# Sorted block attention and a gated feed-forward on one core: a written list of calls with one score block of chunks 3 and 4 a layer ahead, eight 64-row score blocks, and narrower warm-up products

## The chip, the cores and the metric

The kernel runs on one core of a Trainium2 chip. The metric is the device time of one execution, in microseconds (us); before the change the median of three runs is 238.9 us (238.58 to 239.17). The engines are named as the profile names them: PE (TensorE, the matmuls), PEld (its weight loads), DVE (VectorE), ACT (ScalarE), POOL (GpSimd) and SP (SyncE, here only a queue that issues transfers).

## The reference

Queries, keys and values are (4, 8, 768, 64): four batches, eight heads, 768 positions in 8 blocks of 96. A small matrix per head sorts (mixes) the key and value blocks, attention runs within each block of 96, and the result goes through a feed-forward layer with a cosine gate.

```python
P = sort_net                                  # (4, 8, 8, 8)
for _ in range(5):
    P = exp(P - max(P)); P /= sum over the last axis; P /= sum over the axis before
k_sorted = einsum('bhij,bhjcd->bhicd', P, k blocks)
v_sorted = einsum('bhij,bhjcd->bhicd', P, v blocks)
attn = softmax(q block @ k_sorted block.T / 8)     # 96 x 96, within a block
x    = (attn @ v_sorted block)                     # all heads: 3072 tokens x 512
h    = x @ w_in                                    # 512 -> 2048
out  = (h * cos(h)) @ w_out                        # 2048 -> 512
```

## The kernel before

The 3072 tokens are handled in eight chunks n = 0 to 7 of 384 tokens; a chunk has four units u = 0 to 3, each one block of 96 positions with all its eight heads. In the text a letter and the numbers n, u stand for one step; the list of calls after the change uses the same letters.

The feed-forward of a chunk, here called its layer, is eight up steps and twelve down quarters. An up step U n p (function `up`) is 8 products of 384 columns into PSUM, followed by C (the cosine on ACT, written as a sine with a bias) and G (the multiplication on DVE). A down quarter D n t q is 4 products of 512 columns (line 583); there are three row tiles t with four quarters each, then an eviction O and a store W. The time in which the down quarters run is called the layer's tail.

The attention of chunk n+1 is put between the products of layer n. For a unit: S, the scores, 8 products of 96 columns over 128 rows (line 405, in `qk`, or in halves of four products, `qk_half`); M, the row maximum, and X, its subtraction (DVE, lines 447 and 449); E, the exponential on ACT (`expo`, line 467) into one of three buffers `p_buf`; TD, a transpose by DMA on SP's queue into `pT` (or TP and TE: on PE with an eviction, `p_transpose`); AV, 8 products of 65 columns (`av_products`, line 514); N, a reciprocal and a multiplication on DVE (lines 525 and 527) giving `xn`; and XD, a transpose by DMA into the next layer's `xT` (or XP and XE on PE with an eviction, `x_transpose`, line 545).

The sorting of keys and values is made of products too: `ks` and kg (`k_sort_g`) for keys, vb (`v_sort_b`) and vg (`v_sort_g`, 128-column products) for values, each with an eviction (kge, vbe, vge). Two transfers on SP (kswap) exchange halves of the sorted keys.

PSUM is held in two pools: `big`, three buffers of two banks, and `acc`, two buffers of one bank. A buffer is given to the next tile that asks for it in the order of the program, so that a product waits for the reader of the tile that was there before: for a G, an X, an N or an eviction.

Nothing reorders the work at run time: each engine runs its instructions in the order of the program. Before the change, nested calls set this order: `moe_up` and `moe_down` take lists of calls (slots) that are made behind a step, for example

```python
    moe_up(3, [[(w_next,), (qk_half, 4, 0, 0)], [(w_next,)],
    ...
               [(w_next,), (qk_half, 4, 1, 1)], [(qk, 4, 2)]])
    moe_down(3, [[(qk, 4, 3), (expo, 4, 2)], [(w_next, A, *B), (qk, 5, 0), (expo, 4, 3)],
```

At the start, while inputs are loaded and the Sinkhorn iterations run on DVE and ACT, `keep_warm` issues products of zeros on PE (line 238).

Of the kernel before, what the change touches and what calls it, by code (L numbers as in the profile page):

```python
# [14 lines left out]
AX = mybir.AxisListType  # L15


@with_exitstack
def kernel(
# [15 lines left out]
    nc = tc.nc  # L35
# [199 lines left out]

    def keep_warm(times, t, cols=512):
        for _ in range(times):
            nc.tensor.matmul(  # L238
                t[:, :cols], warm[:], warm[:, :1].to_broadcast([128, cols]),
                start=True, stop=True)  # L240
# [131 lines left out]
    MH = H2 * IC  # L372

    def k_products(ps, t, c, rows, rhs, keys=kbuf):
        nc.tensor.matmul(  # L375
            ps[:, t], keys[rows, c * 2 * D:(c + 1) * 2 * D], rhs, start=True, stop=True)

    def k_sort_g(t0, eng, pool, tag):
        ps = pool.tile([128, 4, 4 * NB], FP32, name="ks", tag=tag)
        for t in range(4):  # L380
            k_products(ps, t, t0 + t, slice(0, 128), bds[1].rearrange("p x i -> p (x i)"),
                       pair)
# [25 lines left out]
    def v_cols(d, permuted):  # L408
        return vperm[:, d * blk:d * blk + 128] if permuted else vv[:, d]

    def v_sort_b(b, d0, nd, eng, pool, tag):
        ps = pool.tile([128, nd, 2 * NB], FP32, name="vs", tag=tag)
        rows, xs = slice(0, 64 + b * 64), slice(b * H, (b + 1) * H)
        for t in range(nd):
            nc.tensor.matmul(
                ps[:, t], v_cols(d0 + t, b == 1 or d0 + t >= D // 2)[rows],
                bdv[rows, xs].rearrange("p x i -> p (x i)"), start=True, stop=True)
        copy_on(
            eng, vS[0][:, b * 2 * NB:(b + 1) * 2 * NB, d0:d0 + nd],
            ps[:blk].rearrange("p t n -> p n t"))  # L420

    def v_sort_g(d0, nd, eng, pool, tag):
        ps = pool.tile([128, nd, 4 * NB], FP32, name="vs", tag=tag)
        for t in range(nd):
            nc.tensor.matmul(  # L425
                ps[:, t], v_cols(d0 + t, True), bds[1].rearrange("p x i -> p (x i)"),
                start=True, stop=True)
        copy_on(eng, vS[1][:, :, d0:d0 + nd], ps[:blk].rearrange("p t n -> p n t"))

    def v_at(g, b2, hp, h2, i):  # L430
        return (b2 * 2 + hp) * NB + h2 * nb + i


    LATE = 5
    s_t, pb, pT, xn_t = {}, {}, {}, {}
    xT = {}
    cnt = [0]

    def qk_part(n, u, part, pool, tag):
# [7 lines left out]
        nc.vector.reduce_max(mx[:], scv, axis=AX.X)  # L447
        s = s_t[n, u][:, part[0]:part[0] + w].rearrange("p e h c -> p (e h) c")
        nc.vector.tensor_tensor(s, scv, mx.to_broadcast(list(s.shape)), op=ALU.subtract)  # L449
# [12 lines left out]
    def expo(n, u, on_pe=False):
        p = p_bufs[cnt[0] % NP]
        cnt[0] += 1


        nc.scalar.activation(  # L467
            p[:, :, :blk], s_t.pop((n, u)).rearrange("p e h c -> p (e h) c"), AF.Exp,
            scale=scale)
        if n < LATE:  # L470
# [30 lines left out]

    def av_products(n, u):
        g, b2, ih = where(n)
        if n not in xT:
# [14 lines left out]
        av_ps[n, u] = a  # L519

    def av_norm(n, u, on_pe=False):
        avv = av_ps.pop((n, u))[:blk, :, :H2 * (D + 1)].rearrange(
# [3 lines left out]
        xn = small.tile([blk, H2, 2, D], BF16, name="xn", tag="xn")  # L526
# [3 lines left out]
        if on_pe:  # L530
            xn_t[n, u] = xn
        else:
            nc.sync.dma_start_transpose(
                out=xT[n][:, :, u * blk:(u + 1) * blk],
                in_=xn.rearrange("p h e d -> p (h e d)"))

    def x_transpose(n, u, eng, pool, tag, to=None):
        us = range(u, (u if to is None else to) + 1)
        ps = pool.tile([128, KC, len(us), blk], BF16, name="xps", tag=tag)

        turn = order[:] if n < NQ else ident[:blk, :blk]
        for i, z in enumerate(us):
            xn = xn_t.pop((n, z))
            for h2 in range(H2):
                nc.tensor.transpose(
                    ps[:, h2, i], xn[:, h2].rearrange("p e d -> p (e d)"), turn)
        copy_on(eng, xT[n][:, :, u * blk:us.stop * blk], ps.rearrange("p k i c -> p k (i c)"))

    gt = {}

    def up(n, fp):
        w = TC

        h = big.tile([128, 2, 512], FP32, name="h", tag="big")
        for f2 in range(2):
            f = fp * 2 + f2
            for kk in range(KC):
                nc.tensor.matmul(  # L558
                    h[:, f2, :w], w_in_t[:, kk, f * 128:(f + 1) * 128], xT[n][:, kk],
                    start=(kk == 0), stop=(kk == KC - 1))  # L560
        c = cosp.tile([128, 2, TC], FP32, name="c", tag="c")
        nc.scalar.activation(c[:], h[:, :, :w], AF.Sin, bias=half_pi[:, 0:1])  # L562
        if fp % 2 == 0:
# [3 lines left out]
            gt[n, fp // 2][:, f:f + 2], c[:], h[:, :, :w], op=ALU.mult)  # L567

    out_ps, kept = {}, {}

    def store(n, ts, o_s, eng=nc.sync):
        r0 = n * TC + ts * 128
        eng.dma_start(out=out[r0:r0 + 128, :], in_=o_s[:])

    def let_go(n, ts):
        store(n, ts, kept.pop((n, ts)))

    def down(n, ts, half, stores, mid=()):
        if half == 0:
            out_ps[ts] = acc.tile([128, Dm], FP32, name="o", tag="acc")  # L580
        o = out_ps[ts]
        for f in range(half * FC // 2, (half + 1) * FC // 2):
            nc.tensor.matmul(  # L583
                o[:], gt[n, f // 4][:, f % 4, ts * 128:(ts + 1) * 128], w_out_t[:, f, :],
                start=(f == 0), stop=(f == FC - 1))
            if f % (FC // 2) == FC // 4 - 1:
                step(mid)
        if half == 0:
            return
        if stores is None:  # L590

            z = (n % 2 * 3 + ts) * 2 * Dm
            o_s = vbuf[:, z:z + 2 * Dm].bitcast(FP32)
        else:
            o_s = op.tile([128, Dm], FP32, name="o_s", tag="o_s")
        late = n > 0 and ts == TC // 128 - 1
        copy_on(V if late else A, o_s[:], o[:])
# [542 lines left out]
```

## Time and profile before

| what | value |
|---|---|
| time, median of three runs | 238.9 us (238.58 to 239.17) |
| the profiled execution: its span | 236.9 us; no time of its own is given for it, so the 2.0 us between the span and the median stand for what lies around it |
| PE busy | 228.3 us, 96% of the span |
| DVE, ACT, POOL busy | 171.1 us (72%), 154.0 us (65%), 93.4 us (39%) |
| mean granted TensorE clock | 0.998 |
| layer 1's tail (72.82 to 87.91 us) | 15.09 us, PE busy 14.80 |
| layer 2's tail (100.43 to 115.54 us) | 15.11 us, PE busy 14.69 |
| layer 3's tail (128.63 to 142.54 us) | 13.91 us, PE busy 13.50 |

A row of the profile's timeline is "start, length, engine, line, operation, tile written <- tiles read, count", and in square brackets the idle time before it and what ended it. The modelled end of a matmul lies behind the start of the next, so that the real step of a product is the difference of two starts divided by the count between them, and a wait is what such a difference has beyond that.

### The profile page before, as it was taken

The numbers are of one execution on the slowest core, as the hardware profiler recorded it, in microseconds if no ns is written. First come the engines' busy times: TensorE is split into PE (matmuls) and PEld (weight loads), VectorE is DVE, ScalarE is ACT, GpSimd is POOL, SyncE is SP. The second block draws the span as 40 slices with busy tenths as digits, with TensorE's granted clock in tenths as the row PEclk, the third lists the DMA queues.
The fourth block names the chain that finished last, engine by engine and source line by source line (L and its number), as shares of the span: only waits on it lengthen the run. The fifth ranks groups of instructions, "written<-read, shape, count | busy, mean of one in ns | idle before, by whom it ended". The sixth has DMA issues, their size and how long they took to land.

```text
span 236.9 us, 5429 instructions
## 1 busy us (share of the span) xinstructions
PE 228.3 (96%) x2230; PEld 144.0 (61%) x2230; DVE 171.1 (72%) x284; ACT 154.0 (65%) x205; POOL 93.4 (39%) x117
## 2 busy tenths in 40 slices
PE   8699999999999999999999999999999999999994
PEld 2368799567665656655666556655564565555553
DVE  5658976887789666893689976998698769535700
ACT  3356975588889747795688747673767376646611
POOL 7699994894970098940808000800000000000000
PEclk9999999999999999999999999999999999999999
DMA  7999999995899989869899938944972460341012
GB/s 97 203 199 205 203 224 211 148 201 167 102 117 183 146 155 136 160 150 184 95 104 101 116 64 150 209 68 91 119 216 46 80 192 3 55 133 47 0 44 89
DMA packets 66423, 30.89 MB, mean 130 GB/s; under 512 B 55136, under 2 KB 61920, under 8 KB 66144
## 3 DMA queue, kind: packets, MB, share of 16 engines
q0 software_dynamic: 24048, 13.64, 42.1%
q1 hardware_dynamic: 42064, 16.73, 33.4%
q8 instruction: 17, 0.28, 0.5%
q10 hardware_dynamic: 288, 0.20, 0.3%
q14 instruction: 6, 0.05, 0.1%
HBM read 27.27 MB, written 6.29 MB: 142 GB/s over the span
## 4 chain that ended last, share of the span: by engine, by line
PE 81%; DMA 6%; ACT 4%; DVE 4%; issue 3%; POOL 1%; SPq 0%; ACTq 0%; POOLq 0%
PE h L558 31%; PE o L583 21%; DMA pT<-p_buf 5%; PE h L735 5%; PE o L756 4%; PE sc L405 3%; PE av L514 3%; PE ks L375 2%; PE vs L662 2%; ACT p_buf L467 2%; PE o L1104 1%; PE vs L425 1%; PE pps L713 1%; DMA xT<-xn 1%; PE vs L238 1%
## 5 line engine op out<-in xcount | busy, mean ns | idle before, releaser
L558 PE MATMUL h<-xT,w_in_t 128*128 128x384 bf16 x448 | 78.4, 326 | 0.2 <-DMA xT<-xn 0.2
L583 PE MATMUL o<-w_out_t,gg 128*128 128x512 bf16 x320 | 76.5, 379 | 0.0
L566 DVE TENSOR_TENSOR gg<-c,h 128x768 bf16<-128x768 f32 x56 | 52.6, 949 | 18.8 <-ACT c L562 18.8
L562 ACT ACTIVATE c<-h,half_pi 128x768 f32<-128x768 f32 x56 | 50.4, 900 | 22.5 <-PE h L558 21.6
L558 PEld LDWEIGHTS <-w_in_t 128*128 128x128 bf16 x448 | 42.2, 98 | 26.5 <-issue 0.6
L583 PEld LDWEIGHTS <-gg 128*128 128x128 bf16 x320 | 29.1, 98 | 27.6
L467 ACT ACTIVATE p_buf<-s 96x768 bf16<-96x768 f32 x32 | 26.0, 840 | 4.4 <-DVE s L702 2.4
L179 POOL COPY vperm<-kv 64x1536 bf16<-64x1536 bf16 (+1 forms) x10 | 28.0, 2831 | 0.6 <-DMA kv<-in_v_dram 0.6
L449 DVE TENSOR_TENSOR s<-sc,mx 96x384 f32<-96x384 f32 (+1 forms) x33 | 24.3, 735 | 1.8
L447 DVE TENSOR_REDUCE mx<-sc 96x4 f32<-96x384 f32 (+1 forms) x33 | 24.0, 729 | 0.7 <-PE sc L405 0.7
L527 DVE TENSOR_TENSOR xn<-av,r 96x512 bf16<-96x512 f32 x32 | 22.0, 687 | 1.1
L525 DVE RECIPROCAL r<-av 96x8 f32<-96x8 f32 x32 | 6.4, 199 | 14.6 <-PE av L514 14.4
L129 POOL DMA_DIRECT2D kv<-in_q_dram x24 | 15.9, 674 | 0.7 <-issue 0.5
L405 PE MATMUL sc<-kTs,q_turned 128*128 128x96 bf16 x224 | 15.3, 206 | 0.1
L249 ACT COPY kv<-o 128x512 f32<-128x512 f32 (+2 forms) x10 | 5.3, 530 | 14.9 <-PE o L583 12.4
L405 PEld LDWEIGHTS <-q_turned 128*128 128x128 bf16 x224 | 12.6, 98 | 4.0 <-DVE s L449 0.4
L249 ACT CAST kTs<-ks 128x512 bf16<-128x512 f32 (+1 forms) x18 | 11.0, 632 | 5.7 <-PE ks L375 5.7
L756 PE MATMUL o<-w_out_t,gg 128*128 128x512 bf16 x48 | 11.4, 379 | 0.0
L251 DVE COPY kv<-o 128x512 f32<-128x512 f32 (+1 forms) x5 | 3.0, 602 | 11.4 <-PE o L1104 8.5
L129 POOL DMA_DIRECT2D q_mem<-in_q_dram x16 | 10.7, 684 | 1.2 <-DMA kv<-in_v_dram 1.0
L238 PE MATMUL idle<-warm 128*128 128x512 bf16 x29 | 8.5, 436 | 2.8 <-ACT q_turned L321 1.8
L735 PE MATMUL h<-xT,w_in_t 128*128 128x192 bf16 x128 | 11.1, 246 | 0.0
(119 smaller groups left out, 285.0 us busy)
## 6 DMA issues: line engine op xcount, KB each, us to landing
out_dram<-kv SPq DMA_DIRECT2D x12, 256.0 KB, 2.5
out_dram<-o_s SPq DMA_DIRECT2D x10, 256.0 KB, 2.7
w_in_t<-in_moe_w_in_dram POOLq DMA_DIRECT2D x4, 512.0 KB, 11.8
w_out_t<-in_moe_w_out_dram POOLq DMA_DIRECT2D x4, 512.0 KB, 12.6
kv<-in_k_dram POOLq DMA_DIRECT2D x2, 768.0 KB, 10.3
kv<-in_v_dram POOLq DMA_DIRECT2D x2, 768.0 KB, 13.1
pair<-in_k_dram POOLq DMA_DIRECT2D x2, 768.0 KB, 11.0
kv<-in_v_dram POOLq DMA_DIRECT2D x6, 256.0 KB, 5.4
```

Of the source, the lines that this page charges most:

```text
L129: nc.gpsimd.dma_start(out=q_heads[:, i, :, e], in_=src[:, ih * IC + i, :, e])
L179: nc.gpsimd.tensor_copy(dst, src)
L405: nc.tensor.matmul(out, q_of(n, hp)[:, x:x + 128], keys_of(n, u, h2, hp), start=True, stop=True)
L447: nc.vector.reduce_max(mx[:], scv, axis=AX.X)
L449: nc.vector.tensor_tensor(s, scv, mx.to_broadcast(list(s.shape)), op=ALU.subtract)
L467: nc.scalar.activation(p[:, :, :blk], s_t.pop((n, u)).rearrange("p e h c -> p (e h) c"), AF.Exp, scale=scale)
L527: nc.vector.tensor_tensor(xn.rearrange("p h e d -> p e h d"), avv[:, :, :, :D], r.to_broadcast([blk, 2, H2, D]), op=ALU.mult)
L558: nc.tensor.matmul(h[:, f2, :w], w_in_t[:, kk, f * 128:(f + 1) * 128], xT[n][:, kk], start=(kk == 0), stop=(kk == KC - 1))
L562: nc.scalar.activation(c[:], h[:, :, :w], AF.Sin, bias=half_pi[:, 0:1])
L566: nc.vector.tensor_tensor(gt[n, fp // 2][:, f:f + 2], c[:], h[:, :, :w], op=ALU.mult)
L583: nc.tensor.matmul(o[:], gt[n, f // 4][:, f % 4, ts * 128:(ts + 1) * 128], w_out_t[:, f, :], start=(f == 0), stop=(f == FC - 1))
L735: nc.tensor.matmul(o[:, part, f2 * w:(f2 + 1) * w], w_in_t[:, kk, f * 128:(f + 1) * 128], xT[0][:, kk, h * w:(h + 1) * w], start=(kk == 0) ...
```

## The change

The nested calls are replaced by a table of some 800 lines, `PLAN`, which a loop reads; every function is cut into its parts (S, M, X, E, TD, AV, N, XD and so on), so that each part has a place of its own. In the head, up to about 57 us, every engine has the same order as before but for the warm-up products. Behind it:

- Unit 0 of chunk 3 gets its scores in layer 1's tail (S 3 0) and unit 0 of chunk 4 in layer 2's tail (T 4 0), a layer earlier than before; T 5 0 goes ahead of D 3 0 0. The transposed probabilities of units 0 and 1 of chunks 3 and 4 are put into `kbuf`, which is free by then, not into `pT`.
- Eight units, T 3 3, 4 0, 4 3, 5 0, 6 1, 6 2, 7 0 and 7 1, have products over 64 rows, which is half of the rows each, in pairs into two banks. Two of the value sorts (vgT 0 and vgT 2) have two 64-row products of 64 columns where there was a 128-row product of 128: 16 each where there were 8.
- Two units fewer have `xn` transposed on PE: units 0 and 1 of chunks 3 and 4 go by DMA (XD), units 2 and 3 on PE.
- Some up steps and down quarters change places: layer 1 runs U 0, 1, 3, 2, 4 and on, layer 4 U 1, 2, 0, 3, 5, 4, layer 7 U 0, 5, 2, 1, 4, 3.
- The first eighteen warm-up products are cut into four each and the nineteenth into two (`MORE = 55`): 55 more by the program's order, of the same columns in sum. PE's program has 4588 rows where it had 4462: 110 for these 55 and their weight loads, 32 for the value sorts, and 16 fewer for `xn`.

DVE in layer 1's up steps. `gg` is a G, `mx` an M, `s` an X, `vS<-vs` the eviction of a value sort. Before, from the second G on:

```order
L566 TENSOR_TENSOR gg_1295<-c_1330,h_1321 128x768
L447 TENSOR_REDUCE mx_1349<-sc_1344 96x4
L449 TENSOR_TENSOR s_1343<-sc_1344,mx_1349 96x384
L566 TENSOR_TENSOR gg_1363<-c_1361,h_1352 128x768
L566 TENSOR_TENSOR gg_1363<-c_1384,h_1375 128x768
L447 TENSOR_REDUCE mx_1402<-sc_1397 96x4
L449 TENSOR_TENSOR s_1343<-sc_1397,mx_1402 96x384
L566 TENSOR_TENSOR gg_1416<-c_1414,h_1405 128x768
L566 TENSOR_TENSOR gg_1416<-c_1437,h_1428 128x768
L447 TENSOR_REDUCE mx_1446<-sc_1441 96x4
L449 TENSOR_TENSOR s_1440<-sc_1441,mx_1446 96x384
L566 TENSOR_TENSOR gg_1470<-c_1468,h_1459 128x768
```

After, from the second G on:

```order
L1499 TENSOR_TENSOR gg_1363<-c_1385,h_1376 128x768
L1360 TENSOR_REDUCE mx_1424<-sc_1419 96x4
L1499 TENSOR_TENSOR gg_1426<-c_1417,h_1408 128x768
L1360 TENSOR_REDUCE mx_1455<-sc_1439 96x4
L1374 TENSOR_TENSOR s_1457<-sc_1439,mx_1455 96x384
L1499 TENSOR_TENSOR gg_1426<-c_1437,h_1428 128x768
L1374 TENSOR_TENSOR s_1457<-sc_1419,mx_1424 96x384
L1071 CAST vS_109<-vs_1461 96x64x8
L1499 TENSOR_TENSOR gg_1471<-c_1453,h_1444 128x768
L1499 TENSOR_TENSOR gg_1471<-c_1492,h_1483 128x768
L1360 TENSOR_REDUCE mx_1500<-sc_1495 96x4
L1374 TENSOR_TENSOR s_1502<-sc_1495,mx_1500 96x384
```

Before, each half of a unit has its M and its X side by side, behind two G. Now the M of the half that is scored first stands ahead of a G, the second half's M and X follow, and the first half's X comes only after another G; the eviction of vb 4 (`vS<-vs`) stands on DVE behind both.

ACT in layer 2's tail. `p_buf` is an E, the casts to `pair` are evictions of value sorts, `o_s<-o` an O. Before:

```order
L467 ACTIVATE p_buf0_106<-s_1759 96x8x96
L467 ACTIVATE p_buf1_107<-s_1850 96x8x96
L249 COPY o_s_1949<-o_1918 128x512
L467 ACTIVATE p_buf2_108<-s_1927 96x8x96
L249 CAST pair_89<-vs_1968 96x128x8
L467 ACTIVATE p_buf0_106<-s_1952 96x8x96
L249 CAST pair_89<-vs_1999 96x128x8
L249 COPY o_s_2017<-o_1978 128x512
L249 CAST pair_89<-vs_2048 96x128x8
L249 CAST pair_89<-vs_2093 96x128x8
```

After:

```order
L1378 ACTIVATE p_buf1_107<-s_1845 96x8x96
L1378 ACTIVATE p_buf2_108<-s_1936 96x8x96
L1378 ACTIVATE p_buf0_106<-s_1998 96x8x96
L1069 CAST pair_89<-vs_2010 96x128x8
L1069 CAST pair_89<-vs_2062 96x128x8
L1069 COPY o_s_2133<-o_2057 128x512
L1069 CAST pair_89<-vs_2148 96x128x8
L1378 ACTIVATE p_buf1_107<-s_2109 96x8x96
L1069 CAST pair_89<-vs_2182 96x128x8
```

The three E of chunk 3 that are left there (units 1, 2, 3) stand together ahead of the first value eviction, where an O and a value eviction stood between the second, third and fourth E; the E of unit 0 is a layer earlier, and that of chunk 4's unit 0 stands now among the last evictions.

SP's queue in the same tail: the two transfers of kswap, the TDs (`<-p_buf`), the stores and the XDs (`xT<-xn`). Before:

```order
L388 DMA kTs_98<-kTs_98 64x3072
L389 DMA kTs_98<-kTs_98 64x3072
L480 DMA_TRANSPOSE pT_1913<-p_buf0_106 128x8x96
L480 DMA_TRANSPOSE pT_1916<-p_buf1_107 128x8x96
L573 DMA out_0_dram<-o_s_1949 128x512
L480 DMA_TRANSPOSE pT_1966<-p_buf2_108 128x8x96
L480 DMA_TRANSPOSE pT_1988<-p_buf0_106 128x8x96
L573 DMA out_0_dram<-o_s_2017 128x512
L533 DMA_TRANSPOSE xT_2020<-xn_2032 128x4x96
```

After:

```order
L1244 DMA kTs_98<-kTs_98 64x3072
L1245 DMA kTs_98<-kTs_98 64x3072
L1396 DMA_TRANSPOSE kv_87<-p_buf1_107 128x8x96
L1396 DMA_TRANSPOSE pT_1994<-p_buf2_108 128x8x96
L1396 DMA_TRANSPOSE pT_2027<-p_buf0_106 128x8x96
L1445 DMA_TRANSPOSE xT_2043<-xn_2041 128x4x96
L1550 DMA out_0_dram<-o_s_2053 128x512
L1445 DMA_TRANSPOSE xT_2043<-xn_2118 128x4x96
L1550 DMA out_0_dram<-o_s_2133 128x512
```

The TD of unit 0 is gone from here (it stands a layer earlier), those of units 1, 2 and 3 follow each other with no store between them, unit 1's into `kbuf` (named `kv`), and there are two XDs where there was one.

The diff, cut to its core:

```diff
+MORE = 55
+PLAN = """\
...
+S 2 0 c 1
+M 2 0 1
+G 1 3
+U 1 2
+C 1 2
+S 2 0 c 0
+U 1 4
+C 1 4
+M 2 0 0
+X 2 0 0
+G 1 2
+X 2 0 1
+vb 4 c
...
+T 3 3 B
+E 3 1 1
+TD 3 1
...
+T 4 3 B
+T 5 0 B
...
     def keep_warm(times, t, cols=512):
         for _ in range(times):
-            nc.tensor.matmul(
-                t[:, :cols], warm[:], warm[:, :1].to_broadcast([128, cols]),
-                start=True, stop=True)
+            n = 1 + min(3, pieces[0])
+            pieces[0] -= n - 1
+            for i in range(n):
+                c = slice(i * cols // n, (i + 1) * cols // n)
+                nc.tensor.matmul(
+                    t[:, c], warm[:], warm[:, :1].to_broadcast([128, c.stop - c.start]),
+                    start=True, stop=True)
...
+    def vgT(z, nd, pool, tag):
+        o = kept_tile(("vg", z), pool, tag, [128, 2, nd, 2 * NB], FP32, "vs")
+        for t in range(nd):
+            for b in range(2):
+                rows = slice(b * 64, (b + 1) * 64)
+                nc.tensor.matmul(
+                    o[:, b, t], v_cols(z * 4 + t, True)[rows],
+                    bds[1][rows, b * H:(b + 1) * H].rearrange("p x i -> p (x i)"),
+                    start=True, stop=True)
...
+    def T(n, u, pool, tag):
+        o = kept_tile(("s", n, u, None), pool, tag, [128, 2, 512], FP32, "sc")
+        for h2 in range(H2):
+            for hp in range(2):
+                rows, x = slice(hp * D, (hp + 1) * D), (u * H2 + h2) * blk
+                nc.tensor.matmul(
+                    o[:, hp, h2 * 128:h2 * 128 + blk], q_of(n, hp)[rows, x:x + 128],
+                    keys_of(n, u, h2, hp)[rows], start=True, stop=True)
...
+    def p_to(n, u):
+        if n < LATE and (n < 3 or u > 1):
+            t = ptp.tile([128, 2 * H2, blk], BF16, name="pT", tag="pT")
+        elif n < LATE:
+            z, w = 2 * (QZ + D), 2 * H2 * blk
+            t = kbuf[:, z + u * w:z + (u + 1) * w].rearrange("p (a c) -> p a c", c=blk)
...
+    for line in PLAN.split("\n"):
+        name, *args = line.split()
...
+        calls[name](*given)
```

More of the change, by code (lines that the diff above doesn't have):

```diff
@@ new lines @@
+U 2 2
+G 2 1
+C 2 2
+kg 8 c
+kge 8 A
+G 2 2
+S 3 1 c 1
+M 3 1 1
+X 3 1 1
+U 2 3
+C 2 3
+kg 9 c
+G 2 3
+U 2 4
+kge 9 A
+C 2 4
+G 2 4
+kg 10 c
+kge 10 A
+S 3 2 c 0
+U 2 5
+M 3 2 0
+X 3 2 0
+C 2 5
+G 2 5
+kg 11 c
+kge 11 A
+kswap 1
+U 2 6
+S 3 2 c 1
+M 3 2 1
+U 2 7
+C 2 6
+G 2 6
+C 2 7
+G 2 7
+T 3 3 B
+E 3 1 1
+TD 3 1
+X 3 2 1
+E 3 2 2
+TD 3 2
+M 3 3
+X 3 3
+D 2 0 0
+D 2 0 1
+E 3 3 0
+vgT 0 8 B
+TD 3 3
+ones 1
+AV 3 0
+N 3 0
+XD 3 0
+D 2 0 2
+D 2 0 3
+O 2 0 o V
+W 2 0
+vge 0 8 A
+D 2 1 0
+vgT 2 8 B
@@ new lines @@
+E 5 1 0
+E 5 0 2
+XD 4 1
+TD 5 0
+TD 5 1
+QD 6
+D 3 1 2
+D 3 1 3
+AV 4 2
+N 4 2
+D 3 2 0
+AV 4 3
+N 4 3
+O 3 1 v A
+D 3 2 1
+D 3 2 2
+XP 4 2 B
+XE 4 2 A
+hq 0
+Lq 7
+XP 4 3 B
+XE 4 3 V
+D 3 2 3
+O 3 2 v V
+U 4 1
+U 4 2
+C 4 1
+G 4 1
+C 4 2
+S 5 2 c 1
+S 5 2 c 0
+W 3 0
+M 5 2 1
+M 5 2 0
+G 4 2
+X 5 2 0
+U 4 0
+C 4 0
+G 4 0
+W 3 1
+W 3 2
+U 4 3
+C 4 3
+G 4 3
+U 4 5
+C 4 5
+G 4 5
+X 5 2 1
+U 4 4
+C 4 4
+G 4 4
+U 4 6
+U 4 7
+C 4 6
+G 4 6
+C 4 7
+S 5 3 B
+M 5 3
+G 4 7
+E 5 2 1
+TD 5 2
+D 4 0 0
+AV 5 0
@@ L372, with kept_tile @@
     MH = H2 * IC
[L374 to L381, printed above, removed]
+    ps, made = {}, {}
+    def kept_tile(key, pool, tag, shape, dtype, name):
+        ps[key] = pool.tile(shape, dtype, name=name, tag=tag)
+        return ps[key]
@@ L566, in up @@
         nc.vector.tensor_tensor(
[L567 to L597, printed above, removed]
-        if stores is None or stores == "held":
-            kept[n, ts] = o_s
-        else:
-            store(n, ts, o_s, nc.sync if late else stores)
```

1447 lines of the change are left out of this document (911 added, 536 removed).

## The prediction

> **What bounds the kernel now.** I read the page first: the busy share of each engine and the chain that ended last.
>
> ```profile
> PE 228.3 (96%) x2230; PEld 144.0 (61%) x2230; DVE 171.1 (72%) x284; ACT 154.0 (65%) x205; POOL 93.4 (39%) x117
> ...
> q8 instruction: 17, 0.28, 0.5%
> ...
> PE 81%; DMA 6%; ACT 4%; DVE 4%; issue 3%; POOL 1%; SPq 0%; ACTq 0%; POOLq 0%
> ...
> L566 DVE TENSOR_TENSOR gg<-c,h 128x768 bf16<-128x768 f32 x56 | 52.6, 949 | 18.8 <-ACT c L562 18.8
> L562 ACT ACTIVATE c<-h,half_pi 128x768 f32<-128x768 f32 x56 | 50.4, 900 | 22.5 <-PE h L558 21.6
> ```
>
> PE bounds it. Only two things can shorten the span: fewer PE steps, or fewer waits between them. So the second view was the chain in order of time, for the real step of each kind of product, and the timeline of PE for the waits.
>
> ```profile
> 14.26 0.32 PE ks L238
> ...
> 18.82 0.24 PE sc L681 x13
> ...
> 58.00 0.84 PE ks L375 x24
> 58.84 0.83 PE qps L260 x32
> ...
> 61.08 0.47 PE vs L415 x16
> 61.55 1.30 PE h L558 x8
> ...
> 72.98 1.73 PE o L583 x8
> 74.71 0.34 PE sc L405 x8
> ```
>
> A 512-column product takes 1.73/8 = 0.216 us, a 384-column one 0.162, a 96-column one 0.042, a 64-column one 0.47/16 = 0.029. From 58.00 to 58.84 there are 24 such 64-column products, 0.68 us by that step: 0.16 us is a wait. The biggest waits, where layers 1, 2 and 3 end:
>
> ```profile
> 86.27 0.34 PE L545 MATMUL xps<-order,xn 96*128 96x96 bf16 x4
> 86.87 0.34 PE L545 MATMUL xps<-order,xn 96*128 96x96 bf16 x4 [0.27 <-DVE xn L527]
> ...
> 108.91 0.68 PE L514 MATMUL av<-vS,pT 96*128 96x65 bf16 x16
> 109.94 0.61 PE L425 MATMUL vs<-bd,vperm 128*128 128x128 bf16 x8 [0.34 <-ACT pair L249]
> ...
> 139.12 0.51 PE L545 MATMUL xps<-ident,xn 96*128 96x96 bf16 x8
> 140.03 0.43 PE L514 MATMUL av<-pair,pT 96*128 96x65 bf16 x8 [0.41 <-DMA pT<-p_buf]
> ```
>
> Four products of 0.042 from 86.27 end at 86.44, so 0.43 us go there; 16 of 0.029 from 108.91 end at 109.38, so 0.51 beyond the handover; eight from 139.12 end at 139.46, so 0.57. The second waits for ACT, which itself was held:
>
> ```profile
> 100.63 0.90 ACT L562 ACTIVATE c<-h,half_pi 128x768 f32<-128x768 f32 x1 [0.57 <-PE h L558]
> 101.55 1.28 ACT L467 ACT_TABLE_LOAD   x1
> 102.85 1.58 ACT L467 ACTIVATE p_buf<-s 96x768 bf16<-96x768 f32 x2
> ...
> 108.13 0.84 ACT L467 ACTIVATE p_buf<-s 96x768 bf16<-96x768 f32 x1 [1.47 <-DMA pT<-p_buf]
> 108.88 1.00 ACT L249 CAST pair<-vs 96x1024 bf16<-96x1024 f32 x1
> ```
>
> The fourth E of layer 2's tail needs the `p_buf` that an earlier TD was still reading, and the eviction for which PE waits stands behind it. Why are the TDs late? The chain and the DMA queues (in the windows 131.4 to 133 and 137.5 to 140) say:
>
> ```profile
> 131.57 2.83 DMA pT<-p_buf
> ...
> 134.49 0.85 ACT p_buf L467
> ...
> 135.62 4.37 DMA pT<-p_buf
> ```
>
> ```profile
> q1 hardware_dynamic: 145, 0.04, 12.8%
> ...
> q1 hardware_dynamic: 795, 0.19, 39.0%
> q8 instruction: 1, 0.02, 2.2%
> ```
>
> The same 96x768 transpose takes 2.83 us with no packet of the instruction queue, and 4.37 us when one falls into it: 1.54 more. The page counts 17 of them, and PE has 4460 matmuls and loads, so one comes about every 262 PE instructions (4460/17). That is a second lever: 110 PE instructions more in the head bring each of them forward by 110 instructions, up to 110/16 x 1.30 = 8.9 us in the up steps (16 instructions a step).
>
> The Trainium skill (Runtime: NRT & Kernel Launch, section Instruction fetch mechanics) says that instructions are refilled in blocks of 256 and that crossing a boundary is mostly hidden. The block agrees with the 262 here; the "hidden" does not hold for a transpose in flight (4.37 against 2.83).
>
> **The change part by part.** *Waits that go.* (1) 0.57 at 140.03: with T 4 3 and T 5 0 ahead of layer 3's down quarters the three E of chunk 4 stand together, so that the third ends at C 0.95, table load 1.28 and 3 x 0.84 = 4.8 us behind the last up product and its TD lands at 7.6; AV 4 3 comes on PE behind nine quarters (7.8), the two T (0.6), three AV (0.7) and S 5 1 (0.34), at 9.4. Even a long landing of 1.54 more would be covered. (2) 0.51 at 109.94: E 3 0 is a layer earlier, only three E are left for three buffers, and the evictions are no longer behind an E that waits. (3) 0.43 at 86.87: XP 2 3 comes now behind D 1 2 2 and two more transposes, over 0.86 us after its place before. (4) Ten smaller ones, 1.63 in sum, of which 0.16 at 58.84 is the first and the last is this (181.81 + 7 x 0.216 = 183.32, 0.08):
>
> ```profile
> 181.81 1.67 PE L583 MATMUL o<-w_out_t,gg 128*128 128x512 bf16 x7
> 183.40 0.43 PE L514 MATMUL av<-pair,vperm 96*128 96x65 bf16 x8
> ```
>
> Most of these go because a product that was next in line has now another in front of it; together with the three above, -3.14.
>
> *Work that goes.* Eight products for `xn`: 8 x 0.042 = -0.34. Their two XDs run on SP's queue behind the TDs, and are wanted only by the next layer's first up step; two of DVE's or ACT's evictions go with them.
>
> *64 rows.* A T needs four pairs instead of eight products: if a pair costs one product, 4 x 0.042 = 0.17 less; eight times -1.34. A vgT: eight pairs of 64 columns, 8 x 0.029, against eight of 128, which take 113.07 - 112.62 = 0.45 in the rows below: -0.21 each, -0.42. That pairs run together is seen in chunk 0: 13 products of 64 rows in 0.24 us, 0.018 each, below the 0.029 of a single one. Going over to 64 rows and back costs: the 512-column product at 14.26, which stands between 64-row products, takes 0.32 instead of 0.216, 0.10 each way. Six visits (T 3 3; vgT 0; vgT 2 with T 4 0; T 4 3 with 5 0; T 6 1 with 6 2; T 7 0 with 7 1) cost +1.20. Net -0.57. By 0.018 a product, scaled to 96 columns (0.028), a T would save only 0.12 and the net would be -0.06; I take -0.57, since the 0.24 holds the way out of the mode too. T 3 3 and vgT 0 alone save nothing.
>
> ```profile
> 112.62 0.61 PE L425 MATMUL vs<-bd,vperm 128*128 128x128 bf16 x8
> 113.07 1.03 PE L583 MATMUL o<-w_out_t,gg 128*128 128x512 bf16 x4
> ```
>
> The Trainium skill speaks against such single visits: TensorEngine Tiling (Array Packing), Key Properties, says that a change of the tiling mode drains TensorE. The 0.32 row agrees, and its price, 0.10, is what stands in the sum.
>
> *Moved ahead.* S 3 0 in layer 1's tail adds nothing that wasn't done in layer 2; its M and X (2 x 0.95) fall into DVE's gaps while PE runs down quarters; its E goes to ACT between two key evictions. One more TD on SP's queue there has four stores and two kswap transfers of layer 2 behind it; nobody waits for them within 5 us.
>
> *New waits.* DVE's rows for M and X, whole and by halves:
>
> ```profile
> L449 DVE TENSOR_TENSOR s<-sc,mx 96x768 f32<-96x768 f32 x15 | 14.3, 954 | 1.2
> L447 DVE TENSOR_REDUCE mx<-sc 96x8 f32<-96x768 f32 x15 | 14.2, 947 | 0.7 <-PE sc L405 0.7
> L449 DVE TENSOR_TENSOR s<-sc,mx 96x384 f32<-96x384 f32 x18 | 10.0, 553 | 0.6
> L447 DVE TENSOR_REDUCE mx<-sc 96x4 f32<-96x384 f32 x18 | 9.8, 547 | 0.0
> ```
>
> (a) Layer 1: both `acc` buffers are held by the halves of S 2 0, and vb 4 waits for X 2 0 0. Counted from the start of U 1 0: PE wants vb 4 at 7.76 (five up steps of 1.30, four vb of 0.23, two halves of 0.17); DVE ends G 1 3 at 6.75, then M 0.55 and X 0.55: 7.85 and the handover, so +0.1 to 0.3; I take 0.3. (b) U 1 5 then waits for G 1 2's buffer: 7.85 + 0.95 = 8.80 against PE's 8.4: +0.4. (c) AV 3 1 waits: C 2 7 ends 0.95 behind the last up step, a table load and E 3 1 bring 3.2, TD 3 1 lands at 6.0 by the 2.83; PE is there at 5.7 (five quarters 4.3, T 3 3 0.3, vgT 0 0.33, AV 3 0 0.25, vgT 2 with T 4 0 0.5): +0.3. (d) T 5 0 waits for G 3 6: +0.24. (e) In layer 4's tail AV 5 3 waits for X 6 1, +0.15, and U 5 1 for XD 5 2, +0.25, where U 5 0 waited 0.33. Sum +1.64. Each hangs on one DVE or ACT instruction more or less: bounds 0 and 0.95 apiece, 0 to 5.7 for the six. I stay near the worked value, because the counts above come from the rows of the same engines in the same loops.
>
> *The head.* Cutting a 512-column product in four costs 4 x 0.055 against 0.216, under 0.01 each; PE idles there anyway, so I take 0, with bounds of -0.1 and +0.3 should that cover go:
>
> ```profile
> PE idle L238 <- ACT q_turned L321: 1.8, 2, 1.3
> ```
>
> Sum: -3.14 - 0.34 - 0.57 + 1.64 = -2.4. Against the profiled execution's span of 236.9 this gives 234.5; the median of the runs lies 2.0 above the span, so 236.5.
>
> **The rivals.** *Fetches land in the new transposes.* The TDs that matter are TD 3 1 (already 0.3 late by (c)) and TD 4 1, which lands 5.9 behind the last up step, 0.3 before AV 4 1 wants it. A hit costs 1.54 on the first and 1.24 on the second, and a third on chunk 5's as much: 4.3, so 240.8; two give 239.3. By the order after, the tenth and twelfth fetch fall 60 and 40 PE instructions ahead of these TDs, while the point at which a fetch comes varies by some 70 from one to the next before. It decides from 3.1 us of hits. If the skill's "hidden" held, this case would not exist, and the sum would stay 236.5.
>
> *DVE becomes the bound in the up steps.* If each of the six places in (a) to (e) waits a whole G, +5.7 instead of +1.64: 238.9 - 4.05 + 5.7 = 240.5, slower; half of that surplus gives 238.5, no change. It decides from a mean wait of 0.8 each. For it speaks that DVE holds PSUM longer in layers 1 and 3, where more attention is done; against it that DVE is busy 72% of the span and G itself mostly waits for ACT.
>
> *The reordering only moves the waits.* Of -3.14 only the three big ones, -1.51, have a cause that the change removes; the ten smaller ones may come back elsewhere: 238.9 - 1.51 - 0.91 + 1.64 = 238.1. *Mode changes dearer*: 0.2 each way makes +1.2, 237.7. Both are still faster.
>
> **How the numbers follow.** A measurement of this kernel tells 0.3% (0.7 us) from no change. The forecast (-3.3 to -1.3): 0.56; waits that only move or dearer modes (-1.3 to -0.7): 0.19; half of DVE's surplus, or one hit and one of these: 0.11, no change; hits at three places or DVE the bound: 0.14, slower. Faster 0.75, same 0.11, slower 0.14. The range, 235.3 to 239.2, leaves out about 0.08 below (all new waits nothing: 234.9) and 0.11 above.
>
> **What would show it.** In the profile after: no wait of over 0.2 us on `pT` at layer 3's end or on an eviction of value sorts in layer 2's tail; E of chunk 3 without idle time before it; transposes at 2.8 to 3.1 us from issue in the tails of layers 2 and 3; layer 3's tail about 12.0 us from its first down quarter to U 4's first; in layer 1 a wait for an X before a `vs` and for a `gg` before an `h`. A transpose of over 4 us ahead of AV 3 1 or AV 4 1, or waits of PE on G in every layer, would make the prediction wrong.

## The result and the profile after

The changed kernel takes 236.66 us in the median of six runs (236.52 to 237.13), the kernel before 239.03 in the median of six; the ratio is 0.9889, with a 95% interval of 0.9863 to 0.9915. Forecast were 236.5 us and a range of 235.3 to 239.2. The profiled execution took 237.13 us, the longest of the six, with a span of 235.3, 1.6 below the 236.9 of before. In each of the six 1.7 to 1.8 us lie between span and time, so the 2.0 us set down for it before the change were 0.2 too many.

The page after, the rows that answer to those of before:

```profile
PE 226.5 (96%) x2270; PEld 146.0 (62%) x2293; DVE 172.3 (73%) x287; ACT 151.3 (64%) x201; POOL 93.8 (40%) x117
...
q8 instruction: 18, 0.29, 0.5%
...
PE 82%; DMA 7%; ACT 3%; POOL 3%; DVE 2%; issue 2%; POOLq 0%
...
L1499 DVE TENSOR_TENSOR gg<-c,h 128x768 bf16<-128x768 f32 x56 | 53.0, 949 | 22.4 <-ACT c L1493 22.3
L1493 ACT ACTIVATE c<-h,half_pi 128x768 f32<-128x768 f32 x56 | 50.5, 901 | 25.5 <-PE h L1487 23.3
```

PE is the bound as before, there is one instruction fetch more (18 packets), ACT has 2.7 us less work and DVE 1.2 us more. (The trace lacks 23 matmul records: 2270 beside 2293 weight loads. Rows with a count that is short by one are no wait.)

The busy time by stretches, from the first product of layer 1 on: length of the stretch, then PE, PEld, DVE, ACT and POOL busy, and at the end the granted clock, the share of the DMA engines and GB/s. The stretches are the up steps and the tail of layers 1, 2 and 3 in turn; the cuts at 73.66 and 101.12 stand ahead of a half score block and of T 3 3, which come before the first quarter.

```profile
59.96:73.66 13.70, 13.28 (x143) 8.67 (x141) 11.19 (x18) 10.74 (x15) 9.98 (x16) 1.00 1.03 125
73.66:88.71 15.05, 14.89 (x156) 9.35 (x156) 12.72 (x22) 11.38 (x18) 5.80 (x10) 1.00 0.91 153
88.71:101.12 12.41, 12.41 (x105) 8.03 (x103) 9.87 (x15) 10.03 (x14) 9.43 (x5) 1.00 1.38 145
101.12:115.76 14.64, 14.16 (x155) 7.90 (x157) 10.39 (x18) 9.93 (x12) 8.83 (x12) 1.00 0.96 170
115.76:129.20 13.44, 13.42 (x125) 8.82 (x124) 10.56 (x15) 11.73 (x17) 6.06 (x10) 1.00 1.12 129
129.20:141.29 12.09, 11.99 (x98) 6.38 (x97) 10.57 (x18) 7.40 (x11) 0.00 (x0) 1.00 0.50 78
```

The tails were 15.09, 15.11 and 13.91 us. Layer 3's tail is 1.8 us shorter, of which 0.7 has only moved ahead into its up steps (T 4 3 and T 5 0 stand there now); layer 2's is 0.5 shorter, layer 1's the same with one score block more in it. (From the first quarter on, as the tails before were taken, they are 14.88, 14.26 and 12.09 us.) Layer 1's first product starts at 59.96 instead of 59.60.

PE's timeline at the places where before the three big waits stood, and where new ones were forecast:

```profile
67.33 0.81 PE L1487 MATMUL h<-xT,w_in_t 128*128 128x384 bf16 x4
68.27 0.64 PE L1268 MATMUL vs<-bdv,vperm 128*128 128x64 bf16 x16
69.13 0.65 PE L1487 MATMUL h<-xT,w_in_t 128*128 128x384 bf16 x3 [0.22 <-DVE gg L1499]
...
87.49 0.51 PE L1457 MATMUL xps<-order,xn 96*128 96x96 bf16 x8
87.83 1.03 PE L1532 MATMUL o<-w_out_t,gg 128*128 128x512 bf16 x4
...
106.87 0.33 PE L1346 MATMUL sc<-kTs,q_turned 64*128 64x96 bf16 x8
107.52 0.43 PE L1423 MATMUL av<-vS,kv 96*128 96x65 bf16 x8 [0.32 <-DMA kv<-p_buf]
...
137.23 1.03 PE L1532 MATMUL o<-w_out_t,gg 128*128 128x512 bf16 x4
138.10 0.42 PE L1423 MATMUL av<-pair,pT 96*128 96x65 bf16 x8
```

At 87.49 eight transposes take 0.34 us, their own time, and AV 4 3 at 138.10 starts four products of 0.216 behind 137.23: the waits of layers 1 and 3 are gone. In layer 2's tail no eviction is waited for any more, but at 107.52 stands a wait that had been forecast: T 4 0's eight 64-row products and the way back end at about 107.0, and AV 3 1 waits 0.52 for TD 3 1. In layer 1 vb 4 starts 0.29 late (four products from 67.33 end at 67.98) and U 1 5 0.38 late.

### The profile page after: what moved, and what is told of

Its sections match the earlier page's. It is cut to its first block, busy times and chain, and to the rows that moved or that the text cites. A ratio compares the mean times of both kernels' runs of the same rounds, so it can differ in the third digit from the quotient of the medians.

```text
span 235.3 us, 5542 instructions
## 1 busy us (share of the span) xinstructions
PE 226.5 (96%) x2270; PEld 146.0 (62%) x2293; DVE 172.3 (73%) x287; ACT 151.3 (64%) x201; POOL 93.8 (40%) x117
## 4 chain that ended last, share of the span: by engine, by line
PE 82%; DMA 7%; ACT 3%; POOL 3%; DVE 2%; issue 2%; POOLq 0%
PE o L1532 32%; PE h L1487 29%; DMA kv<-in_v_dram 5%; PE h L1510 5%; PE av L1423 3%; PE sc L1319 3%; POOL vperm L992 2%; PE ks L1200 2%; PE xps L1457 2%; PE o L1623 2%; PE pps L1405 1%; DMA kv<-p_buf 1%; PE vs L1256 1%; PE vs L1291 1%; ACT c L1493 1%
## 5 line engine op out<-in xcount | busy, mean ns | idle before, releaser
L1532 PE MATMUL o<-w_out_t,gg 128*128 128x512 bf16 x348 | 84.7, 379 | 1.2 <-issue 0.2
L1532 PEld LDWEIGHTS <-gg 128*128 128x128 bf16 x368 | 33.3, 98 | 33.0
L1360 DVE TENSOR_REDUCE mx<-sc 96x8 f32<-96x768 f32 (+1 forms) x41 | 31.5, 771 | 3.1 <-PE sc L1319 1.5
L1058 PE MATMUL idle<-warm 128*128 128x128 bf16 (+2 forms) x83 | 9.5, 288 | 2.2 <-ACT q_turned L1141 1.2
L1071 DVE COPY kv<-o 128x512 f32<-128x512 f32 (+1 forms) x6 | 3.7, 624 | 10.0 <-PE o L1623 6.8
L1319 PE MATMUL sc<-kTs,q_turned 128*128 128x96 bf16 x160 | 11.1, 206 | 0.0
L1058 PEld LDWEIGHTS <-warm 128*128 128x128 bf16 x101 | 8.9, 121 | 3.4 <-issue 1.3
L1319 PEld LDWEIGHTS <-q_turned 128*128 128x128 bf16 x160 | 9.1, 98 | 2.7 <-DVE s L1374 0.2
```

The lines of the kernel that those rows point to most:

```text
L1319: nc.tensor.matmul(out, q_of(n, hp)[:, x:x + 128], keys_of(n, u, h2, hp), start=True, stop=True)
L1360: nc.vector.reduce_max(mx[:], s_view(n, u, hp), axis=AX.XY if n < 2 else AX.X)
L1532: nc.tensor.matmul(out_ps[n, ts][:], gt[n, q][:, f % 4, ts * 128:(ts + 1) * 128], w_out_t[:, f, :], start=(f == 0), stop=(f == FC - 1))
```

## The experiments

They are called e1 to e11. Each ratio is to the kernel before, run beside it; "changed" means the changed kernel, 236.66 us, ratio 0.9889. Waits are differences of starts less the products' own steps.

**Where the fetches fall.** The first two take the new list with fewer of the narrower warm-up products; e1 has none.

```diff
-MORE = 55
+MORE = 0
```

> The new list of calls with the warm-up products whole as before, so 110 PE instructions fewer in the head and each instruction fetch 110 PE instructions later. Theory, fetches lengthen the transposes in flight by 1.5 us: by the trace of the changed kernel the tenth fetch then falls at about 106.8 us into TD 3 1 (lands 107.5), the twelfth at 132.5 into TD 4 1 (134.5), the fourteenth at 162.6 into XD 5 2 (164.2), the fifteenth at 180.4 into TD 6 2 (182.0), each wanted at once by an AV or an up step: 1.3 to 1.5 us each, 240.5 to 242.5 us, slower than the kernel before. Rival one, fetches are hidden and the list alone makes the gain: 236.4 to 236.9. Rival two, the narrower products themselves keep PE better fed in the head: 236.9 to 237.5, with all of the difference ahead of the first up step of layer 1.

Measured: 241.55 us, ratio to before 1.0091 (1.0058 to 1.0123): 4.9 us slower than changed, and slower than before. Four of the eleven executions had a granted clock of 0.991 to 0.993; the other seven have a median of 240.42, 3.8 above changed. The profiled one took 240.22, 3.1 above that of the changed kernel, and this is what its trace can explain. The table of waits names transfers where the changed kernel has one short one:

```profile
PE av L1423 <- DMA pT<-p_buf: 1.5, 2, 1.1
...
PE sc L1346 <- DMA kTs<-kTs: 0.9, 1, 0.9
PE av L1423 <- DMA vperm<-p_buf: 0.7, 1, 0.7
PE av L1423 <- DMA kv<-p_buf: 0.4, 1, 0.4
```

The same in PE's timeline, at the first three:

```profile
79.65 0.39 PE L1200 MATMUL ks<-bd,pair 128*128 128x128 bf16 x4
81.17 0.43 PE L1423 MATMUL av<-vS,pT 96*128 96x65 bf16 x8 [1.13 <-DMA pT<-p_buf]
...
107.69 0.20 PE L1346 MATMUL sc<-kTs,q_turned 64*128 64x96 bf16 x1
108.77 0.33 PE L1346 MATMUL sc<-kTs,q_turned 64*128 64x96 bf16 x7 [0.87 <-DMA kTs<-kTs]
109.51 0.43 PE L1423 MATMUL av<-vS,kv 96*128 96x65 bf16 x8 [0.41 <-DMA kv<-p_buf]
```

And the DMA queues in the windows 78.6 to 78.8 and 106.3 to 106.5, each with the transpose whose issue is under way in it and its time to landing; the third block has the chain's rows for the first of the waits:

```profile
q8 instruction: 1, 0.02, 48.9%
...
pT<-p_buf SPq DMA_TRANSPOSE x1, 4.3
```

```profile
q8 instruction: 1, 0.02, 41.0%
...
kv<-p_buf SPq DMA_TRANSPOSE x1, 4.2
```

```profile
76.46 4.67 DMA pT<-p_buf
...
81.17 0.43 PE av L1423 x8
```

A fetch lies in each window. At 78.7 us both TD 2 0, for which PE waits (issued at 76.46, 4.67 us), and TD 2 1 behind it (4.3) are in flight; TD 3 1 takes 4.2. In sum PE waits 3.8 us more than in the changed kernel: 1.30 for TD 2 0, 1.06 for the key halves, 0.1 more at TD 3 1, 0.5 at TD 4 2, 0.88 in layer 5's tail at TD 6 2. The size was forecast (240.5 to 242.5), the places only in part: TD 2 0 and the transfers of the key halves had not been named, and once these had delayed PE, the later fetches fell elsewhere (XD 5 2 was not hit). Both rivals fall: with the list alone nothing is gained, and the head is no slower without the narrower products (layer 1 starts at 59.48).

And e2:

```diff
-MORE = 55
+MORE = 20
```

> The new list with 20 more warm-up products instead of 55, so each fetch 70 PE instructions later than in the changed kernel. Theory of the fetches: the tenth falls at 104.8 us into TD 3 1 (issued at 104.4), +1.5 on AV 3 1; the twelfth at 130.1, before TD 4 1 is issued, nothing; the fourteenth at 160.1 into TD 5 3, +1.2 on AV 5 3, but not into TD 5 2; the fifteenth at 177.8, before TD 6 2 is issued, nothing: 238.9 to 239.7. Rival, fetches hidden: 236.4 to 236.9. Rival, the number of products counts and not where the fetch falls: between the changed kernel and the run with none of them more, in proportion.

Measured: 239.75 us, 1.0016 (0.9989 to 1.0044). PE waits 1.01 for the key halves, 0.57 for TD 3 1, 0.24 for TD 4 1 and 0.82 in layer 5's tail (the first two in the rows below, where the brackets give only the part behind the modelled end of the product before):

```profile
107.41 0.33 PE L1346 MATMUL sc<-kTs,q_turned 64*128 64x96 bf16 x7 [0.83 <-DMA kTs<-kTs]
108.11 0.43 PE L1423 MATMUL av<-vS,kv 96*128 96x65 bf16 x8 [0.37 <-DMA kv<-p_buf]
```

TD 3 1 was forecast; the key halves, TD 4 1 and layer 5 were not, and TD 5 3 was forecast and not hit, so that 239.75 lies just above the 239.7. 20 of 55 products give 1.8 of the 4.9 us, which in size a mere proportion would explain too; but the waits stand at transfers with a fetch in them, at other places than with none of the products.

**The shift alone, in the old list (e3).** The kernel before with `keep_warm` cut as in the change (the counter starts at 55).

```diff
+    pieces = [55]
     def keep_warm(times, t, cols=512):
         for _ in range(times):
+            n = 1 + min(3, pieces[0])
...
```

> The kernel before with the 55 narrower warm-up products alone, nothing else of the change. Theory of the fetches: the tenth falls at 99 us instead of 106, so the TD that held ACT in layer 2's tail is clean and 0.5 to 0.75 us go there; the twelfth falls at 132.5 into TD 4 0 instead of TD 4 3, 1.2 us later for AV 4 0 and the third buffer, so layer 3's tail gains nothing or loses up to 0.6: 238.2 to 239.3 us. If the shift alone made the gain of the change: 236.6 to 237.3. If the fetches are hidden: 238.9.

Measured: 239.07 us, 0.9989 (0.9964 to 1.0014): no change, within the 238.2 to 239.3 that were expected. PE's timeline in layers 1, 2, 3 and 4:

```profile
63.24 0.40 PE L421 MATMUL vs<-bdv,vperm 128*128 128x64 bf16 x8
64.69 0.33 PE L411 MATMUL sc<-kTs,q_turned 128*128 128x96 bf16 x4 [1.05 <-DMA kTs<-kTs]
...
110.43 0.68 PE L520 MATMUL av<-vS,pT 96*128 96x65 bf16 x16
110.94 0.61 PE L431 MATMUL vs<-bd,vperm 128*128 128x128 bf16 x8
...
140.10 0.51 PE L551 MATMUL xps<-ident,xn 96*128 96x96 bf16 x8
140.44 0.42 PE L520 MATMUL av<-pair,pT 96*128 96x65 bf16 x8
...
161.26 1.03 PE L589 MATMUL o<-w_out_t,gg 128*128 128x512 bf16 x4
163.10 0.43 PE L520 MATMUL av<-pair,vperm 96*128 96x65 bf16 x8 [0.82 <-DMA vperm<-p_buf]
```

The second and third pair are the ones that had waits of 0.51 and 0.57 before: both are gone without any move of work. Two others come instead, 1.21 for the key halves (0.26 before) and 0.98 for TD 5 2, issued at 158.26 and landed at 163.06, each with a fetch in it; TD 4 0 was expected to be hit and was not (the twelfth fetch fell at 129.75, ahead of it). So the shift alone moves the hits to other transfers.

The same with 78 (`pieces = [78]`, e8), to look for a place where none is hit; by the landing above, the TD 5 3 of its text is TD 5 2:

> The kernel before with 78 instead of 55 more, narrower warm-up products: each fetch 156 PE instructions earlier than before. By the trace of the run with 55 the seventh fetch then falls at 59.7 us, ahead of the two transfers between the key halves (from 60.05), the twelfth at 127.7, ahead of chunk 4's TDs, the fourteenth at about 158, where it meets TD 5 0 or 5 1 and no longer TD 5 3. Theory, fetches: the waits of 1.2 and 0.98 of that run go and at most 0.5 comes back: 237.2 to 238.0 us, so that the old list with well-placed fetches gets half of the gain of the change or more, and the list itself is worth about 1 us. Rival, the old list has no gain to get from the fetches: 238.9 to 239.1.

Measured: 238.63 us, 0.9995 (0.9968 to 1.0022), against 237.2 to 238.0 expected. The wait of 0.98 went. The 1.21 became 0.62: the seventh fetch fell at 60.20, behind the issue of the first transfer (59.89) and not ahead of it. And the seventeenth met a transpose in layer 6's tail, where the run before had none:

```profile
207.58 0.81 PE L589 MATMUL o<-w_out_t,gg 128*128 128x512 bf16 x3
210.02 0.43 PE L520 MATMUL av<-pair,vperm 96*128 96x65 bf16 x8 [1.63 <-DMA vperm<-p_buf]
```

By the starts PE waits 1.79 there. The profiled execution took 240.34 us, 1.7 above the median, so that the typical execution probably lacks this hit; none of those was traced.

Without the hits that these runs show, the stretch from layer 1's first product to the last product would be 172.8 us in the kernel before (173.85 less 0.51 and 0.57), 172.5 in the run with 55 (174.42 less 0.95 and 0.98) and 172.9 in the run with 78 (175.09 less 0.36 and 1.79); it is 172.0 in the changed kernel. That puts the list itself at 0.5 to 0.9 us; it is worked out, not measured, since no trace of the old list without hits was found.

**64 rows (e4).** The eight T become S, the two vgT vg; MORE = 71 keeps PE's program at 4588 rows.

```diff
-MORE = 55
+MORE = 71
...
-T 3 3 B
+S 3 3 B
...
-vgT 0 8 B
+vg 0 8 B
```

> The changed kernel with the eight T as S (8 products over 128 rows) and the two vgT as vg, and 71 instead of 55 more warm-up products so that PE's program keeps its 4588 instructions and the fetches their places. By the sum (pairs run together, 0.10 us for each change of mode): +0.57, 237.2 us. If pairs save only what the 13-product row shows (0.12 a T): +0.06, 236.7. If changes of mode cost 0.2 each way: -0.6, 236.0.

Measured: 237.30 us, 0.9911 (0.9878 to 0.9944), 0.6 above changed with intervals that overlap; in the profiles the stretch from layer 1's first product to the last is 172.5 against 172.0. Both agree with the +0.57 of the sum and not with the -0.6 of dearer changes of mode; by the times alone +0.06 could not be ruled out. The rows of the changed kernel speak against it:

```profile
176.14 0.81 PE L1532 MATMUL o<-w_out_t,gg 128*128 128x512 bf16 x3
176.88 0.51 PE L1346 MATMUL sc<-kTs,q_turned 64*128 64x96 bf16 x16
177.33 1.04 PE L1532 MATMUL o<-w_out_t,gg 128*128 128x512 bf16 x4
```

Three products from 176.14 end at 176.79, so that T 7 0 and T 7 1 take 0.54 with both changes of mode, where two S take 0.68. T 3 3 alone takes 0.37 where an S takes 0.34.

**T 4 3 and T 5 0 moved ahead (e10).** They go back behind D 3 0 1.

```diff
-T 4 3 B
-T 5 0 B
 G 3 7
-M 4 3
-X 4 3
...
 D 3 0 0
 D 3 0 1
+T 4 3 B
+T 5 0 B
+M 4 3
+X 4 3
 D 3 0 2
```

> The changed kernel with T 4 3 and T 5 0 (and M and X of unit 3) back behind D 3 0 1, where the kernel before had their scores. If moving them ahead is what freed AV 4 3: E 4 3 is some 0.5 to 1.5 us later, and AV 4 3 waits again, +0.3 to +0.8, 237.0 to 237.5 us. If the wait was only that of the fetch that fell into TD 4 3: AV 4 3 still has its transpose in time, the 0.22 that T 5 0 waits for G 3 6 goes: 236.4 to 236.7.

Measured: 236.49 us, 0.9904 (0.9886 to 0.9922), as expected if the wait was only that of the fetch. AV 4 3 does not wait:

```profile
136.94 1.03 PE L1532 MATMUL o<-w_out_t,gg 128*128 128x512 bf16 x4
137.81 0.42 PE L1423 MATMUL av<-pair,pT 96*128 96x65 bf16 x8
```

Four products of 0.216 lie between 136.94 and 137.81, and nothing else. The move ahead was not what freed it.

**The new waits of layer 1, and two more.** The changed kernel was run again in this group (e5, 236.67 us, 0.9902, 0.9881 to 0.9922):

> The changed kernel once more, as the measure for the other runs of this group on the same chip: 236.4 to 236.9 us.

Then with another order of DVE in layer 1 (e6):

```diff
 M 2 0 1
+X 2 0 1
 G 1 3
...
+G 1 2
 M 2 0 0
 X 2 0 0
-G 1 2
-X 2 0 1
 vb 4 c
-vbe 4 V
 G 1 4
+vbe 4 V
```

> The changed kernel with another order of DVE's M, X and G in layer 1: X 2 0 1 directly behind its M, G 1 2 ahead of the other half, vb 4's eviction behind G 1 4; nothing else moves and PE's program keeps its length. Theory, vb 4 and U 1 5 wait for DVE's order and nothing else: both waits (0.29 and 0.38 in the profile of the changed kernel) go, -0.67, 0.25 to 0.3% faster than the changed kernel: 236.0. Rival, DVE is the bound there and the waits come back one step later: no change, 236.6. With the fetches some 0.6 us earlier against the clock but at the same places of PE's program, no transpose is newly hit.

Measured: 237.19 us, 0.9932 (0.9908 to 0.9956), not faster. vb 4 no longer waits and U 1 5 waits 0.21, but vb 6 waits 1.04 for vb 4's eviction, which now stands behind a G:

```profile
69.71 0.33 PE L1319 MATMUL sc<-kTs,q_turned 128*128 128x96 bf16 x4
70.92 0.39 PE L1268 MATMUL vs<-bdv,vperm 128*128 128x64 bf16 x8 [0.88 <-DVE vS L1071]
```

DVE in the same place:

```profile
69.33 0.94 DVE L1499 TENSOR_TENSOR gg<-c,h 128x768 bf16<-128x768 f32 x1
70.19 0.68 DVE L1071 CAST vS<-vs 96x512 bf16<-96x512 f32 x1
```

The same order (e7), with AV 3 1 behind D 2 2 0 and the first half of S 6 3 ahead of U 5 1:

```diff
 T 4 0 B
-AV 3 1
...
 D 2 2 0
+AV 3 1
...
+S 6 3 c 0
 U 5 1
 C 5 1
-S 6 3 c 0
```

> The order of layer 1 as in the run before, and two more places: AV 3 1 goes behind D 2 2 0, so that TD 3 1 has a quarter (0.86) more; S 6 3's first half goes ahead of U 5 1, which waits for XD 5 2. Theory: the waits of 0.52 and 0.26 in the changed kernel shrink to 0 and 0.09, with layer 1's -0.67 in sum -1.3: 235.3 to 235.5 us. Rival, the next late thing takes over (D 2 2 0 waits for the eviction O 2 0, or fetches fall otherwise): 236.0 to 236.6.

Measured: 236.68 us, 0.9906 (0.9886 to 0.9925), 0.5 below the run without the two (the intervals overlap) and above the 235.3 to 235.5 expected: the wait for TD 3 1 is gone, layer 1's 1.04 stays. In e9, vb 4's eviction stands directly behind X 2 0 0 and vb 5's ahead of G 1 4 in the program:

```diff
 vb 4 c
-G 1 4
 vbe 4 V
 vb 5 B
 vbe 5 A
+G 1 4
```

> The kernel of the two more places (e7), with layer 1 ordered once more: vb 4's eviction directly behind X 2 0 0 and ahead of G 1 4, vb 5's eviction ahead of G 1 4 in the program, so that U 1 6 takes over vb 5's buffer. Theory, each wait in layer 1 is one DVE instruction too early or too late: vb 4, U 1 5 and vb 6 find their buffers free (7.1, 8.05 and 9.84 us behind U 1 0's start, wanted at 7.76, 8.2 and 9.9), -0.67 against the changed kernel there, and -0.6 for AV 3 1 and U 5 1: 235.3 to 235.6 us. Rival, DVE is the bound of layer 1: the wait of 1.04 that stood at vb 6 moves on to U 1 6 or U 1 7 and the time is that of e7, 236.5 to 236.9.

Measured: 236.18 us, 0.9883 (0.9859 to 0.9907). Layer 1's waits are 0.21 (U 1 5) and 0.18 (vb 6) instead of 0.29 and 0.38, and the two other places hold. It lies 0.5 below the changed kernel by the medians and 0.1 by the ratios, less than the expected 1.1 to 1.4, and the intervals overlap.

Last, e11, this kernel with T 4 3 and T 5 0 late:

> The kernel of e9 (layer 1 ordered once more, AV 3 1 behind D 2 2 0, S 6 3's first half ahead of U 5 1) with T 4 3 and T 5 0 behind D 3 0 1 as in e10. If e10's 0.2 and e9's 0.5 are separate waits that end nothing else: 235.9 to 236.1 us, the fastest of all kernels here. If layer 3's tail has no cover left once layer 2 ends earlier: 236.2 to 236.6.

Measured: 236.22 us, 0.9870 (0.9828 to 0.9912). This is not told apart from e9; no kernel here is shown to be faster than the changed one, though both lie 0.4 to 0.5 us below it.

## Why the prediction was right, and where it was not

- *The time.* 236.66 against 236.5: -2.4 against a measured -2.4 by the medians. That the two agree so closely is in part luck. The sum gave a span of 234.5, and the six spans have a median of 234.9; the 2.0 us added for what lies around the span are 1.8, which made up half of the difference. Between the two profiles it is -1.6: the stretch from layer 1's first product on gives -1.86 and the head +0.36.
- *Waits (1) and (2), 0.57 and 0.51.* They went, but not by the cause that was named. With T 4 3 and T 5 0 late (e10) AV 4 3 is still free; with the old list and the shifted fetches (e3) both waits are gone. What held them was a fetch in the transpose (TD 4 3, 4.37 us, and in layer 2's tail the TD whose `p_buf` the fourth E needed, issued at 103.71, 4.33 us with the fetch at 106.04); in the old list it is enough that the fetch falls elsewhere. What moving E 3 0 ahead gave is not shown by itself: e1 has a fetch in the same tail (106.38) and no wait for a value eviction, but waits for the key halves and TD 3 1. The step "even a long landing would be covered" does not hold. In the changed kernel TD 4 3 lands at 137.44, about 9.0 us behind the last up product and not 7.6: the transposes leave SP's queue 1.3 us apart (TD 4 1 to 4 3 at 131.74, 133.07 and 134.38), while the sum counted 0.84 for each E. AV 4 3 comes at 138.10, so that 0.7 us were to spare and not the 1.8 of the working. In e1, where a fetch lies in both TD 4 2 (4.37 us) and TD 4 3 (4.10), AV 4 2 waits 0.50, and AV 4 3, later by as much, starts without a wait of its own.
- *The shift, "a second lever".* It was named with its price for one transpose (1.54), and as a rival where it would hit; in the sum it stood at nothing. That is the term that failed: without it the list is 4.9 us slower (e1), and with it the old list gains nothing (e3). Neither part of the change gains by itself; list and place of the fetches go together. That no fetch met TD 3 1 or TD 4 1 was forecast as the likelier case only: the tenth fetch was over at 103.0 us, 1.4 ahead of TD 3 1, and with 35 warm-up products fewer (e2) it hit.
- *Fetches as a rival.* The mechanism held where a critical transpose was hit: 4.67 us for TD 2 0 and 4.23 for TD 3 1 in e1, 4.79 for TD 5 2 in the old list (e3). The transposes named as the critical ones (TD 3 1, TD 4 1) were only some of them; the transfers of the key halves, TD 2 0, TD 4 2, TD 6 2 and in the old list TD 5 2 were the dearer ones. In the changed kernel the TDs of chunk 3 in layer 2's tail and of chunk 4 in layer 3's take 2.79 to 3.07, as the signs named ahead of the result asked; TD 4 0 and an XD in layer 2's tail take 4.59 and 3.87, but nothing waits for them. By the Trainium skill (Runtime: NRT & Kernel Launch, Instruction fetch mechanics) crossing a block is mostly hidden. For PE's own stream nothing in these runs speaks against it, for transposes in flight the rows of e1 do.
- *Wait (3), 0.43.* Gone, as the row at 87.49 shows.
- *New waits.* (a) 0.29 for 0.3, (b) 0.38 for 0.4, (d) 0.22 for 0.24, (e) 0.26 for 0.25 at U 5 1, while the 0.15 of AV 5 3 did not come and 0.09 stand at AV 5 2; (c) 0.52 for 0.3, since TD 3 1 took 3.07 from the end of its E (the chain's row below) and not 2.83. Sum 1.76 for 1.64. A seventh was not forecast: U 1 1 comes 0.24 late in the changed kernel, since its first weight load waits for DVE's eviction of queries (the last row below, from PE's timeline); with it the sum is 2.00.

```profile
104.41 3.07 DMA kv<-p_buf
...
107.52 0.43 PE av L1423 x8
...
61.95 1.09 PEld L1487 LDWEIGHTS <-w_in_t 128*128 128x128 bf16 x8 [0.19 <-DVE q_turned L1071]
```

- *64 rows.* -0.57 forecast, 0.5 to 0.6 found by undoing it (e4), with overlapping intervals.
- *DVE as the bound.* Not by a whole G at each place; but e6 shows how near layer 1 is to it: one G moved ahead of an eviction made a wait of 1.04.
- *The head.* Taken as 0, bounds -0.1 to +0.3. Layer 1 starts at 59.48 with none or 20 of the narrower products, and at 59.70 to 60.27 in the eight new-list runs with 55 or more, so that they seem to cost 0.2 to 0.8; the same program came to 59.96 and 60.22 in two runs.

## What to carry to other kernels

Where transposes by DMA feed the critical path, find the instruction queue's packets in the trace and see which transposes they fall into: a list of calls and the place of its fetches have to be judged together, since any change in the length of the program ahead moves the fetches behind it. A wait that is gone after a reordering isn't yet explained by it; put the moved piece back alone, and shift the fetches alone. A buffer that is waited for sits behind one instruction of the releasing engine's order, so that moving a reader ahead can hand the wait to the next tile.

## What the runs showed of the hardware

- A 16 KB instruction fetch makes most transposes longer that are in flight with it. In the thirteen traces, from 60 us on and without TD 3 0 and TD 4 0 of the new list, the 202 transposes of 96x768 that have no such packet between issue and landing take 2.77 to 3.38 us; of the 77 that have one, 68 take 3.40 to 5.29 and nine 2.79 to 3.10. The two large transfers between the key halves are held as well: 3.30 and 3.91 us in e3 with the fetch at 60.83 in both, against 2.77 and 2.96 in the kernel before, where a fetch ends 0.4 us behind the issue of the first (PE waits 1.21 and 0.26).
- Not every long landing has a fetch in it: TD 4 0 takes 4.59 us in the changed kernel without one, while loads of the queue q0 run.
- The issue of a transpose occupies SP for 1.2 us, so that three in a row are issued 1.3 us apart (131.74, 133.07 and 134.38 in the changed kernel).
- The price of a fetch was seen at other transfers only, not as a stop of PE itself.
- Going to 64-row products and back costs PE about 0.10 and 0.12 us, so that a single block of eight gains nothing (0.37 for 0.34) and two together gain 0.14.
